# Half of v and k in fp32, the rest by casting loads, and two groups' heads taken to x first: the head of a linear-attention and gated-FFN kernel

## The chip, the cores and the metric

The kernel runs on one core of one Trainium2 chip. The metric is the device time of one execution in microseconds (us), the median of several runs. Five engines work side by side, each through its own list of instructions in order: TensorE (PE in the profile, its weight loads PEld), VectorE (DVE), ScalarE (ACT), GpSimd (POOL) and SyncE (SP). SP and POOL issue the transfers. In this kernel SP's loads keep their type, and POOL's loads convert on the way: fp32 in memory becomes bf16 or fp16 on the chip.

## What is computed

q, k and v are 8 batches x 8 heads x 576 positions x 64, in fp32. The attention is linear, without a softmax:

```python
def phi(x, c, s):
    r = np.maximum(x, 0.0)
    return np.concatenate([r * c, r * s], axis=-1)
q_p = phi(q, cos_w, sin_w)
k_p = phi(k, cos_w, sin_w)
kv = np.einsum('bhsf,bhsd->bhfd', k_p, v)
z = np.sum(k_p, axis=2)
num = np.einsum('bhsf,bhfd->bhsd', q_p, kv)
den = np.einsum('bhsf,bhf->bhs', q_p, z)[..., None] + 1e-06
x = (num / den)            # then 4608 tokens x 512
out = (silu(x @ w_gate) * (x @ w_val)) @ w_out
```

w_gate and w_val are 512 x 1536, w_out is 1536 x 512.

## The kernel before

**Tiles.** The 8 heads of a batch are taken as 4 groups of 2 (`g`), and these as 2 pairs of groups (`j`). A position is a partition p of 64 and a slot c of 9. A tile `t` of x is 128 tokens, two slots of one batch; four tiles make one token group of 512 for the feed-forward part, and there are 9 token groups. The hidden width 1536 is cut into 12 chunks of 128 (`fc`), the model width 512 into 4 (`kc`).

**Three stages.** The head (lines 133 to 563) loads the tables and batch 0 and takes the first four tiles through attention, then the first six chunks of the first token group through the gate (G) and value (V) products, silu (s) and their product (m). From L566 on jobs with costs and due times are planned in Python and put out in the planned order: the rest of the first token group, the other batches, the token groups 1 to 8 (with a scheme of seven products in place of eight on sums of blocks of x and of the weights) and the stores. The last stage ends with the stores of the last token group.

**What sets the order of the head.** The list `words` (L501) is an order written out by hand. Each word is one step, and the engine of a step gets its instructions in the order of the words: `tm` and `te` spread the tangents over the partitions and copy them out, `cq` casts two slots of q, `tq` turns a tile of q on TensorE, `qr` is its relu, `qw` its product with the tangents, `rk` the relu of k, `kv` the products of k with v times (cos, sin), `kvo` their copies to SBUF, `a` the products of a tile of q with kv, `den`, `rec` and `x` the denominator, its reciprocal and the quotient, `xt` and `xc` the turn of x on TensorE and the copy of it, `z` products of zeros with nobody to read them (`idle_products`, L184), `WG` and `WV` sums of weight blocks. A number behind the point is a part of a step or, for G, V, s and m, the tiles that it takes. `@act` and `@dve` choose the engine.

**PSUM.** Its 8 banks are handed out by `take`, the longest unused first; a bank that is held comes back with `give_back`. The planner's first assignment of banks (L1507) starts from the use in the head.

**Loads before.** SP issues six (L158 to L163, `load_first`): v of groups 0 and 1, v of groups 2 and 3, q slots 0 and 1, k of groups 0 and 1, and k of groups 2 and 3 in two parts (slots 0 to 4 and 5 to 8). They stay fp32 and lie in room that is used later for other things (`wo_sb`, `ht`, `wt_sb`). ACT casts v of groups 1 to 3 to bf16 (L461), DVE multiplies v of group 0 straight from fp32 (`vmul`, L293). POOL prepares constants, waits in a copy of one element (`hold`, L467) for the second group of v, and then issues casting loads: q slots 2 and 3, q slots 4 to 7, the first two chunks of w_gate and w_val, each 128 columns, and then the list of L472, larger pieces of the weights, batch 1, w_out and q of batch 2. At most eight of POOL's loads are on their way at a time; a ninth waits for the first.

## Time and profile before

| | us |
|---|---|
| median of 3 runs | 299.42 |
| lowest and highest | 298.96, 299.65 |
| the profiled execution | 298.21 |
| its span, first to last instruction | 296.4 |
| TensorE busy in it | 291.1 |

A line of the timeline begins with the start in us from the span's start and the time in us; then come engine, line of the program, operation, what is written and read, and how many instructions stand together. In brackets stand the idle time of the engine before it and what ended it. The chain of work that ended last is followed back from the last instruction; its pieces are given in order of time with start, length, engine and line. In the rows of slices a digit is a share in tenths. The DMA view gives what the transfers wrote in a stretch of time, and for each group of loads its size and the time from issue to landing.

### The profile page before, as it was taken

How to read it: one execution, taken by the hardware profiler on the slowest of the kernel's cores; microseconds unless marked ns; L12 is line 12 of the kernel's file. 1: busy time of each engine (PE TensorE's matmuls, PEld its weight loads, DVE VectorE, ACT ScalarE, POOL GpSimd, SP SyncE). 2: the span in 40 equal slices, each digit the busy share in tenths (PEclk: the TensorE clock that was granted, in tenths of full speed). 3: DMA queues.
4: the chain of work that ended last, by engine and by line, in shares of the span. 5: the costliest groups of instructions: out<-in, count | busy, mean ns of one | idle time of the engine just before them, and what ended most of it. 6: DMA issues, size and time to landing. Idle time of an engine off the chain costs nothing.

```text
span 296.4 us, 8073 instructions
## 1 busy us (share of the span) xinstructions
PE 291.1 (98%) x3244; PEld 238.7 (81%) x3244; DVE 252.0 (85%) x514; ACT 199.4 (67%) x421; POOL 69.6 (23%) x122
## 2 busy tenths in 40 slices
PE   8999999999999999999999999999999999999994
PEld 4597465776787888898898889888988888888883
DVE  7878997879877999999988987998679868986883
ACT  6564346989559968985699589967465556565630
POOL 7963630003007012221352023200220050002000
PEclk9999999999999999999999999999999999999999
DMA  7999999997989997799996979940470046002026
GB/s 266 225 196 198 202 206 207 203 205 121 194 177 144 229 190 122 151 171 149 174 203 133 186 113 162 183 81 2 107 110 2 0 97 119 2 0 73 0 58 157
DMA packets 71973, 40.89 MB, mean 138 GB/s; under 512 B 48768, under 2 KB 68736, under 8 KB 71936
## 3 DMA queue, kind: packets, MB, share of 16 engines
q0 software_dynamic: 24800, 24.39, 49.1%
q1 hardware_dynamic: 46528, 15.47, 28.9%
q10 hardware_dynamic: 608, 0.52, 0.7%
q8 instruction: 25, 0.41, 0.6%
q14 instruction: 12, 0.10, 0.1%
HBM read 37.75 MB, written 9.44 MB: 159 GB/s over the span
## 4 chain that ended last, share of the span: by engine, by line
PE 97%; DVE 1%; issue 0%
PE banks L977 45%; PE banks L1142 24%; PE banks L1052 5%; PE banks L1262 4%; PE banks L438 4%; PE banks L904 4%; PE banks L187 3%; PE banks L716 3%; PE banks L785 2%; PE banks L779 1%; PE banks L372 1%; PE banks L1310 0%; PE banks L315 0%; PE banks L418 0%; PE banks L351 0%
## 5 line engine op out<-in xcount | busy, mean ns | idle before, releaser
L1111 POOL DMA_DIRECT2D out_dram<-ob x52 | 27.3, 532 | 104.8 <-ACT ob L630 69.7
L1036 ACT ACTIVATE sg<-banks 128x512 bf16<-128x512 f32 x72 | 41.3, 599 | 5.6 <-PE banks L977 5.4
L977 PEld LDWEIGHTS <-wg_sb 128*128 128x128 f16 x384 | 36.9, 98 | 6.3
L628 ACT COPY banks<-banks 128x512 f32<-128x512 f32 (+1 forms) x53 | 29.9, 572 | 17.5 <-PE banks L977 7.3
L1142 PEld LDWEIGHTS <-ht 128*128 128x128 f16 x384 | 37.4, 98 | 4.8
L1072 DVE TENSOR_TENSOR ht<-sg,banks 128x512 f16<-128x512 bf16 x60 | 39.9, 680 | 0.9 <-PE banks L977 0.6
L977 PEld LDWEIGHTS <-wgs_sb 128*128 128x128 f16 x368 | 35.7, 98 | 4.6
L997 DVE TENSOR_TENSOR banks<-m,banks 128x512 f32<-128x512 f32 x44 | 30.2, 693 | 10.6 <-ACT m L628 8.1
L977 PEld LDWEIGHTS <-wv_sb 128*128 128x128 f16 x320 | 31.0, 98 | 3.8
L977 PE MATMUL banks<-kvt,wgs_sb 128*128 128x256 f16 x236 | 33.4, 273 | 0.0
L1142 PEld LDWEIGHTS <-sums 128*128 128x128 f16 x288 | 27.9, 98 | 3.3
L630 ACT ACTIVATE ob<-banks 128x512 f32<-128x512 f32 x32 | 18.8, 596 | 15.9 <-PE banks L1142 15.2
L977 PE MATMUL banks<-xT,wg_sb 128*128 128x256 f16 x192 | 28.8, 273 | 0.0
L628 ACT COPY m<-banks 128x512 f32<-128x512 f32 x44 | 25.5, 590 | 4.4 <-PE banks L977 4.3
L1142 PE MATMUL banks<-wo_sb,ht 128*128 128x256 f16 x192 | 25.7, 273 | 0.0
L1142 PE MATMUL banks<-wt_sb,sums 128*128 128x256 f16 x192 | 24.9, 273 | 0.0
L977 PE MATMUL banks<-xT,wv_sb 128*128 128x256 f16 x160 | 24.0, 273 | 0.0
L1036 ACT ACTIVATE sg<-m 128x512 bf16<-128x512 f32 x24 | 15.1, 630 | 12.4 <-DVE m L1005 12.2
L807 DVE TENSOR_TENSOR x<-banks,rec 128x512 f16<-128x512 f32 x32 | 21.6, 686 | 1.5 <-DVE rec L803 0.2
L977 PE MATMUL banks<-kvt,wg_sb 128*128 128x256 f16 x168 | 22.4, 273 | 0.0
L1142 PE MATMUL banks<-wt_sb,ht 128*128 128x256 f16 x192 | 22.3, 273 | 0.0
L877 ACT ACTIVATE r_q<-raw_q,tanq 128x256 bf16<-128x256 bf16 x45 | 20.7, 510 | 0.1
(160 smaller groups left out, 544.7 us busy)
## 6 DMA issues: line engine op xcount, KB each, us to landing
out_dram<-ob POOLq DMA_DIRECT2D x52, 128.0 KB, 3.9
raw_kv<-in_k_dram POOLq DMA_DIRECT2D x7, 576.0 KB, 5.9
raw_q<-in_q_dram POOLq DMA_DIRECT2D x12, 288.0 KB, 10.7
raw_kv<-in_v_dram POOLq DMA_DIRECT2D x6, 576.0 KB, 8.3
out_dram<-ob SPq DMA_DIRECT2D x12, 128.0 KB, 2.5
wg_sb<-in_moe_w_gate_dram POOLq DMA_DIRECT2D x5, 256.0 KB, 8.9
wv_sb<-in_moe_w_val_dram POOLq DMA_DIRECT2D x5, 256.0 KB, 9.5
wo_sb<-in_v_dram SPq DMA_DIRECT2D x2, 576.0 KB, 4.2
```

The lines of the kernel that those rows point to most:

```text
L438: nc.tensor.matmul(out=st["f", tg, fc, lo][i], lhsT=(wg_sb, wv_sb)[i][:, kc, fs], rhs=xT[tg][:, ts, kc], start=(kc == 0), stop=(kc == KC - 1))
L628: nc.scalar.copy(out=out, in_=in_)
L630: nc.scalar.mul(out=out, in_=in_, mul=mul)
L807: tt(out=one(x_all, x).rearrange("p (y e d) -> p e y d", e=2, d=D), in0=view()[:, :, :, 0:D], in1=rec_all[:, t % 4].rearrange("p (e y) o - ...
L877: nc.scalar.activation(out=home()[:, :, c, 1], in_=raws[b, "q"][:, :, c], func=AF.Relu, scale=tanq[:, c:c + 1])
L977: nc.tensor.matmul(out=to[:, i], lhsT=a[:, c, 2 * u + i], rhs=x()[:, :, c], start=first and i == 0 and c == 0, stop=c == KH - 1, skip_grou ...
L997: tt(out=bank(c), in0=one(m7_all, m).rearrange("p i x -> p (i x)"), in1=bank(b), op=ALU.add)
L1036: nc.scalar.activation(out=gates(rooms[w])[:, :, jh * HT:(jh + 1) * HT], in_=src, func=AF.Silu, scale=DOWN)
L1052: nc.tensor.matmul(out=bank(v), lhsT=wv_sb[:, kc, fc * P:(fc + 1) * P], rhs=xT[tg][:, :, kc], start=(kc == 0), stop=(kc == KC - 1))
L1072: tt(out=ht[:, 4 * u + w:4 * u + w + 3:2, jh * HT:(jh + 1) * HT], in0=gates(rooms[w])[:, :, jh * HT:(jh + 1) * HT], in1=src.rearrange("p ( ...
L1111: {"POOL": nc.gpsimd, "SP": nc.sync, "ACT": nc.scalar}[j.eng].dma_start(out=out_v[idx // NC, idx % NC][:, cols], in_=ob_of(t)[e * SH:(e + ...
L1142: nc.tensor.matmul(out=to, lhsT=a[:, kc, i * P:(i + 1) * P], rhs=b[:, kc], start=first and kc == 0 and i == 0, stop=kc == HC - 1, skip_gro ...
```

## The change

- v and k of groups 0 and 1 are still loaded by SP in fp32, now each group by itself: two loads of v and four of k (slots 0 to 4 and 5 to 8 of each group). ACT casts both groups of v (`vc`), and DVE multiplies from bf16 (`vm`).
- POOL's wait at L467 goes. POOL issues casting loads at once: q slots 0 to 3, v of groups 2 and 3, k of groups 2 and 3 in two parts, q slots 4 to 7. Behind them stand the weights and the list of before, word for word.
- q has no fp32 part any more: `cast_q` goes, and all turns of q read bf16 from the casting loads.
- Of the first 56 products of zeros 44 go; in the word list three remain (`z3`) of nine.
- The tangents are spread with both halves of the partitions, a diagonal of 320 columns instead of 640.
- Word list: the products kv, the copies, a, den, rec and x of groups 0 and 1 stand first, for tiles 0 and 1 (`HALVED`); then kv of groups 2 and 3, the turns of tiles 2 and 3, and the second halves of tiles 0 and 1. ACT makes the denominators of these four tiles. The first gate and value products take two tiles at once (`01`), and for chunk 0 the lower half of the model width (`Gl`, `Vl`) and the upper one (`Gh`, `Vh`) apart. The copy of x of tile 2 goes to DVE.
- The planner's first assignment of banks is written out (L1507); the order of what follows the word list on TensorE, VectorE, ScalarE and SyncE, and of what POOL issues behind the first weights, is that of before.

The diff, without its unchanged lines:

```diff
...
-    QCUT = 2
+    NW, QCUT = 8, 4
...
-    first = {"q": lodge(G * QCUT * D, FP32).rearrange("p (g c d) -> p g c d", g=G, c=QCUT)}
+    first = {}
...
-    load_first("v", slice(0, 2))
-    load_first("v", slice(2, 4))
-    load_first("q", slice(0, G), 0, 2)
-    load_first("k", slice(0, 2))
-    load_first("k", slice(2, 4), 0, KCUT)
-    load_first("k", slice(2, 4), KCUT, NC)
-    NW = 8
+    for g in range(2):
+        load_first("v", slice(g, g + 1))
+    for g in range(2):
+        load_first("k", slice(g, g + 1), 0, KCUT)
+        load_first("k", slice(g, g + 1), KCUT, NC)
...
-    idle_products(40, 16)
-    idle_products(4)
...
-    tan16 = consts.tile([P, NC + 1], FP16, name="tan16")
+    tan16 = consts.tile([SH, NC], FP16, name="tan16")
+    tan5 = consts.tile([P, (NC + 1) // 2], FP16, name="tan5")
...
-    diag = lodge((NC + 1) * SH, FP16).rearrange("p (c s) -> p c s", c=NC + 1)
+    epd_all = consts.tile([P, NC], FP32, name="eps_down")
+    NH2 = (NC + 1) // 2
+    diag = lodge(NH2 * SH, FP16).rearrange("p (c s) -> p c s", c=NH2)
+    eye2 = consts.tile([P, SH], FP16, name="eye2")
+    nc.vector.tensor_tensor(out=eye2, in0=ident16[:, 0:SH], in1=ident16[:, SH:P], op=ALU.add)
...
-        nc.vector.tensor_tensor(out=tan16[:, 0:NC], in0=csk[:, :, 1], in1=rcos[:, 0], op=ALU.mult)
-        nc.vector.tensor_copy(out=tan16[:, NC:], in_=tan16[:, 0:1])
+        for ps_, at, c0, n in ((slice(0, SH), 0, 0, NH2), (slice(SH, P), 0, NH2, NC - NH2), (slice(SH, P), NC - NH2, 0, 1)):
+            nc.vector.tensor_tensor(out=tan5[ps_, at:at + n], in0=csk[ps_, c0:c0 + n, 1], in1=rcos[ps_, 0, c0:c0 + n], op=ALU.mult)
...
+        nc.vector.tensor_single_scalar(out=epd_all, in_=rcos[:, 1], scalar=1e-6 * DOWN, op=ALU.mult)
...
-        nc.vector.tensor_tensor(out=diag[0:SH], in0=ident16[0:SH, 0:SH].unsqueeze(1).to_broadcast([SH, NC + 1, SH]),
-                                in1=tan16[0:SH].unsqueeze(2).to_broadcast([SH, NC + 1, SH]), op=ALU.mult)
+        nc.vector.tensor_tensor(out=diag, in0=eye2.unsqueeze(1).to_broadcast([P, NH2, SH]),
+                                in1=tan5.unsqueeze(2).to_broadcast([P, NH2, SH]), op=ALU.mult)
+        nc.vector.tensor_tensor(out=tan16, in0=csk[0:SH, :, 1], in1=rcos[0:SH, 0], op=ALU.mult)
...
-        nc.tensor.matmul(out=st["tan"][:, 0], lhsT=ones[0:SH], rhs=diag[0:SH, 0:NW].rearrange("p c s -> p (c s)"),
-                         start=True, stop=True)
-        nc.tensor.matmul(out=st["tan"][:, 1, 0:2 * SH], lhsT=ones[0:SH], rhs=diag[0:SH, NW:].rearrange("p c s -> p (c s)"),
-                         start=True, stop=True)
+        for h in range(2):
+            hs = slice(h * SH, (h + 1) * SH)
+            nc.tensor.matmul(out=st["tan"][:, h, 0:NH2 * SH], lhsT=ones[hs], rhs=diag[hs].rearrange("p c s -> p (c s)"),
+                             start=True, stop=True)
...
-        copy_op(eng, tanT.rearrange("p c s -> p (c s)"),
-                st["tan"].rearrange("p b x -> p (b x)")[:, 0:(NC + 1) * SH])
+        copy_op(eng, tanT.rearrange("p (h c) s -> p h (c s)", h=2), st["tan"][:, :, 0:NH2 * SH])
...
-        relu_op(eng, raw_of(0, "k")[:, g, lo:hi], first["k"][:, g, lo:hi])
+        o = raw_of(0, "k")[:, g, lo:hi]
+        relu_op(eng, o, first["k"][:, g, lo:hi] if g < 2 else o)
+
+    cast_v = set()
...
-            in0=(first if b == 0 and g == 0 else {"v": raw_of(b, "v")})["v"][:, g].unsqueeze(2).to_broadcast([P, NC, 2, D]),
+            in0=(first["v"] if b == 0 and g < 2 and g not in cast_v else raw_of(b, "v"))[:, g].unsqueeze(2).to_broadcast([P, NC, 2, D]),
...
-    qf = wgs_sb.rearrange("p n c u x -> p (n c u x)")[:, G * NC * 2 * W:G * NC * 2 * W + 4 * J * D].bitcast(
-        BF16).rearrange("p (c j i d) -> p c j i d", c=2, j=J, i=2)
...
-
-    def cast_q(c, eng):
-        o = qf[:, c % 2].rearrange("p j i d -> p (j i) d")
-        (nc.scalar.copy if eng == "act" else nc.vector.tensor_copy)(out=o, in_=first["q"][:, :, c])
...
-                if t == 0:
-                    nc.tensor.transpose(out=ps[:, y].rearrange("p e s -> p (e s)"),
-                                        in_=qf[:, c, j].rearrange("p i d -> p (i d)"), identity=ident)
-                    continue
...
-                    out=(ps[:, j, 2 * e * D1:2 * (e + 1) * D1] if t == 0 else
+                    out=(ps[:, j, 2 * e * D1:2 * (e + 1) * D1] if t in HALVED else
...
-        if t == 0:
+        if t in HALVED:
...
-    def x_den(t, ps, ys=slice(0, 4)):
-        if ys.start == 0:
-            st["den", t] = den_all[:, t % 4]
-        nc.vector.tensor_scalar(
-            out=st["den", t].rearrange("p (e y) o -> p e y o", e=2)[:, :, ys],
-            in0=a_view(t, ps, ys)[:, :, :, D:D1],
-            scalar1=eps_all[:, 2 * t:2 * t + 1], scalar2=DOWN, op0=ALU.add, op1=ALU.mult)
+    def x_den(t, ps, ys=slice(0, 4), eng=""):
+        st["den", t] = den_all[:, t % 4]
+        o, i_ = st["den", t].rearrange("p (e y) o -> p e y o", e=2)[:, :, ys], a_view(t, ps, ys)[:, :, :, D:D1]
+        if eng == "act":
+            nc.scalar.activation(out=o, in_=i_, func=AF.Identity, scale=DOWN, bias=epd_all[:, 2 * t:2 * t + 1])
+        else:
+            nc.vector.tensor_scalar(out=o, in0=i_, scalar1=eps_all[:, 2 * t:2 * t + 1], scalar2=DOWN,
+                                    op0=ALU.add, op1=ALU.mult)
...
-        if ys.start == 0:
-            st["rec", t] = rec_all[:, t % 4]
-            st["x", t] = x_all[:, t % NX]
+        st["rec", t] = rec_all[:, t % 4]
+        st["x", t] = x_all[:, t % NX]
...
+    HALVED = (0, 1)
...
-    def ffn_mm(tg, fc, lo=0, hi=GH, which=(0, 1)):
+    def ffn_mm(tg, fc, lo=0, hi=GH, which=(0, 1), ks=range(KC)):
...
-        if 0 in which:
+        if 0 in which and 0 in ks:
...
-            for kc in range(KC):
+            for kc in ks:
...
-                                 start=(kc == 0), stop=(kc == KC - 1))
+                                 start=(kc == 0 and (i == 0 or 2 * n > 512)), stop=(kc == KC - 1), skip_group_check=True)
...
+    def load_part(nm, gs, lo, hi):
+        nc.gpsimd.dma_start(out=raw_of(0, nm)[:, gs, lo:hi].rearrange("p g c d -> p g (c d)"),
+                            in_=source(0, nm)[:, gs, lo * D:hi * D])
+
...
-    for g in (0, 1, 2, 3):
-        if g:
-            nc.scalar.copy(out=raw_of(0, "v")[:, g], in_=first["v"][:, g])
-        vmul(0, g)
-        if g == 1:
-            tangent_diagonals()
-    hold = consts.tile([P, 1], FP32)
...
-    nc.gpsimd.tensor_copy(out=hold, in_=first["v"][:, 1, 0, 0:1])
-    load_slots(0, "q", QCUT, 4)
-    load_slots(0, "q", 4, NW)
+    load_part("q", slice(0, G), 0, QCUT)
+    load_part("v", slice(2, 4), 0, NC)
+    load_part("k", slice(2, 4), 0, KCUT)
+    load_part("k", slice(2, 4), KCUT, NC)
+    load_part("q", slice(0, G), QCUT, NW)
...
-    for what in "w2 w4 w6 k w8 s8 w10 v sa o002 o022 sb o044 o084 q2".split():
-        if what[0] == "w":
-            load_w(int(what[1:]))
-        elif what[0] == "o":
-            load_wo(int(what[1:3]), int(what[3:]))
-        elif what == "k":
-            load(1, "k")
-        elif what == "v":
-            load(1, "v", 2)
-        elif what[0] == "q":
-            load_turned(int(what[1:]), "q")
-        else:
-            load_slots(*{"s8": (0, "q", NW, NC), "sa": (1, "q", 0, 3), "sb": (1, "q", 3, NC)}[what])
+
+    def loads():
+        for what in "w2 w4 w6 k w8 s8 w10 v sa o002 o022 sb o044 o084 q2".split():
+            if what[0] == "w":
+                load_w(int(what[1:]))
+            elif what[0] == "o":
+                load_wo(int(what[1:3]), int(what[3:]))
+            elif what == "k":
+                load(1, "k")
+            elif what == "v":
+                load(1, "v", 2)
+            elif what[0] == "q":
+                load_turned(int(what[1:]), "q")
+            else:
+                load_slots(*{"s8": (0, "q", NW, NC), "sa": (1, "q", 0, 3), "sb": (1, "q", 3, NC)}[what])
...
-        tm0 te0@act cq1@act cq0@dve z4 rk1.0@dve rk0.0@act rk3.0@dve rk2.0@dve tq0 z2 rk3.1@dve kv0.0 qr0@act
-        kv1.0 qw0.1 rk2.1@act kvo01@dve kv1.1 tq1 kvo00@act kvo10@dve a0.0 kvo11@act qr1@dve z1 den0.0 qw1.1
-        a0.1 den0.1 tq3 rec0.0 rec0.1 tq2 a1.0 a1.1 z2 x0.0 qr3@act x0.1 den1 xt0.1 qw3.1 xt0.0 rec1 qr2@act
-        xc0.1@act qw2.1 a3.0 x1.0 a3.1 a2.0 den3 xc0.0@act a2.1 G1.0 xt1.0 rec3 G0.0 den2 x3.0 rec2 V0.0
-        xc1.0@act V1.0 s1.0 xt3.0 G0.1 G1.1 V0.1 x2.0 xc3.0@act xt2.0 xc2.0@act s0.1 s0.0 V1.1 G2.01 m0.0
-        s2.01 G3.01 m1.0 WG3.0 WG2.0 WG4.0 G1.23 G3.23 s1.23 V3.23 V1.23 G4.01 s1.1 s3.23 G0.23 m1.23 s3.01 m3.23 m1.1 m0.1
-        WV3.0 WV2.0 WV4.0 s4.01 s0.23 G4.23 G5.23 G2.23 s5.23 G5.01 V2.01 V2.23 V5.23 s4.23 V4.01 m2.01 m5.23 V4.23 s2.23 s5.01
-        m4.01 V3.01 V5.01 m2.23 V0.23 m4.23 m3.01 m5.01 m0.23
+        vc0@act td0 vm0 rk0.0@dve tm0 z3 tq0 vc1@act vm1 qr0@dve te0@act rk1.0@act kv0.0 qw0.1 kvo01@act tq1 vm2 qr1@dve kvo00@act qw1.1 a0.0 rk3.0@act den0.0@act rk2.0@act a1.0 vm3 rk2.1@dve den1.0@act rec0.0 rk3.1@act rec1.0 x0.0 kv1.0 kv1.1 x1.0 tq2 ld0 kvo11@dve kvo10@act tq3 a0.1 xt0.0 a1.1 qr3@act xc0.0@act qr2@dve qw2.1 xt1.0 den1.1@act den0.1@act qw3.1 xc1.0@act rec1.1 a2.0 rec0.1 x1.1 a2.1 den2@act a3.0 a3.1 x0.1 xt1.1 rec2 xt0.1 Gl0.01 xc1.1@act xc0.1@act den3@act x2.0 Vl0.01 G1.01 rec3 Gh0.01 V1.01 Vh0.01 x3.0 G3.01 xt2.0 xt3.0 G2.01 V2.01 xc3.0@act s2.01 WG3.0 xc2.0@dve G0.23 G1.23 s3.01 V1.23 G4.01 G4.23 s0.01 s0.23 s4.01 V0.23 s1.01 s4.23 V4.01 s1.23 m0.01 V4.23 WV3.0 WG2.0 G2.23 V2.23 m1.23 G3.23 m1.01 s2.23 m4.23 m0.23 V3.23 WV2.0 s3.23 m2.23 G5.23 m4.01 G5.01 s5.23 WG4.0 V3.01 WV4.0 V5.23 m3.23 m2.01 m3.01 s5.01 V5.01 m5.23 m5.01
...
-        whole, a, part = b not in ("0", "1") or a != "0", int(a), int(b or 0)
+        whole, a, part = b not in ("0", "1") or int(a) not in HALVED, int(a), int(b or 0)
...
-        elif op == "cq":
-            cast_q(a, eng)
+        elif op == "ld":
+            loads()
+        elif op == "vc":
+            copy_op(eng, raw_of(0, "v")[:, a], first["v"][:, a])
+            cast_v.add(a)
+        elif op == "vm":
+            vmul(0, a)
...
+        elif op == "td":
+            tangent_diagonals()
...
-            x_den(a, st["a", a], ys)
+            x_den(a, st["a", a], ys, eng)
...
-            if op in "GV":
-                ffn_mm(0, a, *span, which=("GV".index(op),))
+            if op[0] in "GV":
+                ffn_mm(0, a, *span, which=("GV".index(op[0]),),
+                       ks={"l": range(KC // 2), "h": range(KC // 2, KC)}.get(op[1:], range(KC)))
...
-    epd_all = consts.tile([P, NC], FP32, name="eps_down")
...
-        free["bank"] = [(t, n) for t, n in zip(BANK_AT, sorted(range(8), key=lambda x: used[x]))]
+        free["bank"] = [(t, n) for t, n in zip(BANK_AT, (0, 4, 5, 7, 2, 1, 6, 3))]
```

## The prediction

> **What bounds the kernel now.** The page comes first: its head, the slices, and the shares of the chain that ended last.
>
> ```profile
> span 296.4 us, 8073 instructions
> PE 291.1 (98%) x3244; PEld 238.7 (81%) x3244; DVE 252.0 (85%) x514; ACT 199.4 (67%) x421; POOL 69.6 (23%) x122
> PE   8999999999999999999999999999999999999994
> PEclk9999999999999999999999999999999999999999
> DMA  7999999997989997799996979940470046002026
> PE 97%; DVE 1%; issue 0%
> ```
>
> TensorE is busy in every slice, and the chain lies on it for 97% of the span. From the profile's end to the run's 298.21 us are 1.8 us that no engine row covers. The diff leaves the order of instructions after the word list as it was on every computing engine, so I ask one thing: when does the first planned product, L904, start? The chain in order of time, cut to that part, says what TensorE does until then.
>
> ```profile
> 0.99 6.88 PE banks L187 x56
> ...
> 10.34 0.65 PE banks L315 x30
> ...
> 13.09 0.57 PE banks L351 x16
> ...
> 14.23 0.43 PE banks L187 x2
> 14.66 0.22 PE banks L418 x4
> ...
> 14.95 1.04 PE banks L372 x15
> ...
> 18.34 8.96 PE banks L438 x84
> ```
>
> L187 is the products of zeros, which fill time. The real work starts near 10 us, and at 15 us the head products of a tile (L372) still stand in front of most feed-forward products (L438). From the timeline I take the pace of the latter and the end of the list:
>
> ```profile
> 18.40 1.91 PE L438 MATMUL banks<-xT,wg_sb 128*128 128x256 f16 x16
> 27.14 0.38 PE L904 MATMUL banks<-xT,wv_sb 128*128 128x512 f16 x1
> ```
>
> One such product lasts 0.27 us alone, so 16 in 1.91 us stand (1.91 - 0.27) / 15 = 0.109 us apart. The planned part starts at 27.14 us. What comes before 10 us waits for data, so the transfers are next: POOL's issues in the timeline, and the DMA view of three stretches.
>
> ```profile
> 2.48 0.81 POOL L179 MEMSET wt_sb<- 128x128 f16 x1
> 5.79 1.68 POOL L129 DMA_DIRECT2D raw_q<-in_q_dram  x2
> DMA packets 2299, 2.73 MB, mean 341 GB/s; under 512 B 501, under 2 KB 1531, under 8 KB 2299
> raw_q<-in_q_dram POOLq DMA_DIRECT2D x1, 256.0 KB, 5.7
> DMA packets 1816, 0.58 MB, mean 182 GB/s; under 512 B 1310, under 2 KB 1816, under 8 KB 1816
> DMA packets 4855, 1.91 MB, mean 191 GB/s; under 512 B 2246, under 2 KB 4853, under 8 KB 4853
> ```
>
> The stretches are 1.8 to 9.8 us (341 GB/s, nearly all fp32), 9.8 to 13 us (182) and 10 to 20 us (191). A casting load is counted by the bf16 or fp16 that it writes, so it reads twice that: 364 and 382 GB/s. Both kinds thus run at about one speed, and the head is a question of how many bytes stand ahead of what. The second q load is issued at about 6.7 us and lands 5.7 us later, at 12.35.
>
> **The change part by part.**
>
> *Loads.* Before, SP brings all of v and k and two slots of q in fp32, and POOL then casts six slots of q. After, SP brings v and k of groups 0 and 1 (four times 288 KB, the k ones each cut in two), and POOL casts q slots 0 to 3 (512 KB read), the rest of v (576), the rest of k (320 and 256) and q slots 4 to 7 (512). SP issues six loads either way; POOL issues five instead of two, 3 x 0.75 us more, but loses the copy of 1.37 us at L467 and its wait, and starts when its memset ends at 2.48 + 0.81 = 3.3 us instead of 5.79. So the weights are issued at about the same time. **Ahead of the last q load's end stand 3,328 KB in both kernels**: 2,304 of v and k and 1,024 of q. SP's 1.18 MB end at 1.8 + 1.18 / 0.341 = 5.3 us. In the old kernel the remaining 2.23 MB end about 0.9 us before 12.35 (the first load of v shows this lag: 0.59 MB at 341 GB/s end at 3.5, and the waiting cast starts at 4.45), that is in 6.15 us; as casting loads at 364 to 382 GB/s they need 5.8 to 6.1. I take 0.25 us of gain, from bounds of 0.0 and 0.35: **q slots 4 to 7 land at 12.1.**
>
> ```profile
> 4.45 0.67 ACT L461 CAST raw_kv<-wo_sb 128x576 bf16<-128x576 f32 x1 [0.64 <-DMA wo_sb<-in_v_dram]
> 69.26 0.75 POOL L121 DMA_DIRECT2D raw_kv<-in_k_dram  x1 [0.40 <-ACT den L797]
> DMA  9998300000000000099957711497999899999999
> q1 hardware_dynamic: 832, 1.11, 105.7%
> ```
>
> That needs the casting queue to be ready when SP's bytes run out. No row shows a casting load this early, so I bound it. With idle engines a load issued at 69.26 moves bytes at about 70.7 (slices of 0.1 us from 69): 1.45 us, hence 4.75 here, before 5.3. On the other side, between 5.8 and 8.8 us only q1, SP's queue, moved anything, though POOL issued at 5.79: 3.0 us, hence 6.3 and a hole of 1.0 us. I take no hole: SP's queue still held work then, so that row shows a turn awaited, not a delay of the load itself.
>
> *Order of the head.* q waits for nothing but its load (the two casts of L339 go), and k, v and the heads of groups 0 and 1 are done while the rest comes in. This removes 50 products of zeros. DVE makes all four products v*table from bf16, ACT makes the denominators (0.27 us each at L797), DVE one copy of x. The tangent set-up gains a few small operations and its diagonal halves; it lies before 6 us, where nothing waits for it longer than for q. None of this is on the path after 12.1, as DVE's and ACT's lists there hold only the following.
>
> ```profile
> 13.48 1.08 ACT L281 ACTIVATE wt_sb<-banks 128x512 bf16<-128x512 bf16 x2 [1.06 <-PE banks L351]
> 14.81 0.65 ACT L323 COPY xT<-banks 128x256 f16<-128x256 f16 x2 [0.24 <-PE banks L418]
> 42.12 0.27 ACT L797 ACTIVATE den<-banks,eps_down 128x8 f32<-128x8 f32 x1 [1.58 <-PE banks L779]
> 13.29 0.29 DVE L397 RECIPROCAL rec<-den 128x4 f32<-128x4 f32 x2
> 13.50 0.74 DVE L401 TENSOR_TENSOR x<-banks,rec 128x256 f16<-128x256 f32 x2
> ```
>
> *The path.* The turns of tiles 2 and 3 stand on TensorE ahead of the second halves of tiles 0 and 1, so these queue behind the landing. From 12.1: 16 transposes 0.57 and a hand-off 0.05; then ACT, in its order: the relu of tile 3 (1.08 / 2), the first xT copy (0.65 / 2), two denominators (0.27 each); then DVE's reciprocal (0.29 / 2) and the two half tiles (0.74); two more hand-offs 0.10, two transposes 0.11. Sum 3.1: the first gate products start at **15.2**. Behind them TensorE has 96 products of 0.109 (10.47) and 8 transposes of 0.22 / 4 (0.44): 26.1. I add 0.2 for a copy that ends 0.1 late behind the half-depth products and a bank not yet free: **26.3, a lead of 0.85 us** on 27.14. Cross-check: from 14.95 the old kernel has the same 96 products' worth (32 of its are half as wide), 15 head products (1.04) and 16 - 4 = 12 transposes (0.66), which gives its 27.1; the new one has 8 transposes (0.44), starts 0.25 later, and so ends 1.0 earlier if nothing waits.
>
> *What could take the lead back.* The weights and W_out are in the same order and bytes. The load of the second weight pair is issued at 10.45 and lands 6.4 later, at 16.85; the new order wants it 16 products (1.74) after 15.2, at 16.95, so it fits only just. W_out's third piece lands at 31.46 + 11.7 = 43.16 and is used at 44.24: 1.08 us of room for a lead of 0.85.
>
> ```profile
> wg_sb<-in_moe_w_gate_dram POOLq DMA_DIRECT2D x1, 256.0 KB, 6.4
> wo_sb<-in_moe_w_out_dram POOLq DMA_DIRECT2D x1, 512.0 KB, 11.7
> 44.24 1.03 PE L1262 MATMUL banks<-wo_sb,ht 128*128 128x512 f16 x4
> ```
>
> Sum: 298.21 - 0.85 = 297.4 for a run like the profiled one. The median of the runs is 299.42, 1.2 us above it; against it the forecast is 299.42 - 0.85 = **298.6 us**.
>
> **The rivals.**
>
> *A hole in the transfers.* If the first casting load comes 1.0 us after SP's bytes end, everything behind it lands 1.0 later, and the path hangs on it: 27.3 instead of 26.3, +0.15 us, **299.6**. For it: q1 alone between 5.8 and 8.8. Against it: the idle-queue row.
>
> *The clock drops (the one that is slower).* The weight loads of the idle products show the price:
>
> ```profile
> 4.81 0.15 PEld L187 LDWEIGHTS <-zeros 128*128 128x128 bf16 x1 [0.28 <-issue]
> 5.22 2.16 PEld L187 LDWEIGHTS <-zeros 128*128 128x128 bf16 x45 [0.26 <-issue]
> ```
>
> Until 5.2 us a product of 512 columns takes 0.43 us, later 0.43 / 2 (L187 x2 above), though PEclk says 9 throughout: TensorE needed 4.2 us of steady work to reach full speed. The new order drops 50 of the filling products and leaves gaps: by my sums the 15 products of zeros end near 6.6, and the first turn waits for q until 7.6 (5.3, then 0.52 MB at 373 GB/s, the middle of the two speeds, then the lag of 0.9); two more gaps of some 0.8 us follow before 12. If the speed falls there, the products from 15.2 on run at half for up to 4.2 us: 2.1 us lost against 0.85 won, **300.7**. It decides once more than 1.7 us of the dense part runs slow. Against it: none of the gaps is long, and TensorE works about half of that time. The Trainium skill ("TensorE: Matmul & The Clock Gate", section "HAM oscillation — how this bites in real kernels") asks for idle gaps above about 3.4 us before the clock falls; by that rule nothing is lost here and the sum stands. The next section of that page ("A second HAM failure mode: psum-queue depth-cycling") tells of many short gaps that did it in another kernel; by that one the time is the rival's. No row here shows a gap in the head of either length.
>
> *The lead isn't kept.* If the casting loads run at 364 and a little less, the weight pairs land 0.3 to 0.6 later than the new order wants them and TensorE waits: lead 0.3, **299.1**.
>
> **How the numbers follow.** A measurement of this kernel tells about 0.2%, 0.6 us, from no change. Forecast 0.54 (0.46 of it faster by more than that, 0.08 within); hole 0.18 (0.10 within, 0.08 slower, as a longer hole adds at once); clock 0.17 (0.02 within, 0.15 slower); lead not kept 0.11 (0.02 faster, 0.09 within). So faster 0.48, within 0.29, slower 0.23. The range goes from 297.8 (no waits, a full 0.35 from the transfers, 1.6 us in all) to 300.6, which takes in the hole and about half of the clock's case.
>
> **What would show it.** Right: the last q load lands near 12.1, the first gate product stands near 15.2, L904's successor starts near 26.3, and later stages are shifted by the same amount. Hole: q0's first packet after 6 us. Clock: 128x256 products 0.22 us apart after 15 us. Lead not kept: waits on weight loads between 16 and 21 us, or on W_out near 43. Wrong in kind would be a changed order after L904, or a slower stage beyond 60 us.

## The result, and the profile after

| | before | after |
|---|---|---|
| median of 6 runs, us | 298.99 | 305.38 |
| lowest and highest | 298.39, 299.65 | 301.76, 309.79 |
| the profiled execution, its span | 298.21, 296.4 | 306.81, 305.0 |

The change makes the kernel slower, by a little over 1%: ratio 1.013, 95% interval 1.009 to 1.017. (The ratio leaves out executions over 1.5% above a kernel's fastest; the medians do not.) The forecast of 298.6 us and its range of 297.8 to 300.6 were missed. What is new beside the time is the spread: 8 us between six runs of the changed kernel, 1.3 between six of the kernel before. (The old kernel isn't free of it: on the chip of a_third two of its 13 runs took 301.7 and 301.9 us, the others 298.0 to 299.1. They weren't traced.) The page of the profiled execution shows two places:

```profile
span 305.0 us, 7963 instructions
PE   8799999999999999999399999999999999999994
PEclk9799999999999999999899999999999999999999
PE 87%; DMA 8%; DVE 1%; POOL 1%; SPq 1%; issue 0%; POOLq 0%
```

TensorE's row, which before has nines between an 8 at the start and a 4 at the end, now has a 7 in the second slice and a 3 in the slice from 145 to 152.5 us. The chain, 97% on TensorE before, now runs through transfers for 8%. The head first, in the timeline of the changed kernel:

```profile
2.58 0.90 POOL L455 DMA_DIRECT2D raw_q<-in_q_dram  x1
...
9.19 0.41 PE L346 MATMUL banks<-ident,raw_q 128*64 128x128 bf16 x8 [1.76 <-DMA raw_q<-in_q_dram]
...
16.97 0.38 PE L434 MATMUL banks<-xT,wg_sb 128*128 128x256 f16 x2
...
19.42 0.61 PE L434 MATMUL banks<-xT,wg_sb 128*128 128x256 f16 x4 [0.54 <-DMA wg_sb<-in_moe_w_gate_dram]
...
28.61 1.03 PE L901 MATMUL banks<-xT,wv_sb 128*128 128x512 f16 x4
```

The first casting load is issued at 2.58, but TensorE waits 1.76 us for it until 9.19; the first gate product stands at 16.97, the second weight pair is waited for at 19.42, and the planned part (L901, once L904) starts at 28.61, 1.47 us later than before. The DMA view of the same kernel, stretch 4.5 to 8.5 us, and the issues of q slots 4 to 7 (at 5.60) and of the second weight pair (at 10.97):

```profile
q0 software_dynamic: 727, 0.49, 89.7%
q1 hardware_dynamic: 336, 0.33, 27.9%
...
raw_q<-in_q_dram POOLq DMA_DIRECT2D x1, 256.0 KB, 8.1
...
wg_sb<-in_moe_w_gate_dram POOLq DMA_DIRECT2D x1, 256.0 KB, 8.4
```

q0 is POOL's queue, which is counted by what it writes: 2 x 0.49 + 0.33 = 1.31 MB were read in these 4 us, where the old kernel read 1.47 MB. q slots 4 to 7 land at 5.60 + 8.1 = 13.7 us instead of 12.35.

The second place is the 3 in the row. TensorE's waits between 30 and 297 us (total, times, longest), and then the chain between 138 and 152 us (start, length, what):

```profile
PE banks L974 <- DMA xT<-x: 5.5, 1, 5.5
```

```profile
138.27 2.08 SPq L744
140.35 0.04 issue
140.39 9.66 DMA xT<-x
150.05 0.05 issue
150.10 1.04 PE banks L974 x4
```

The old kernel has no wait at all in the first of these views. Here SP issues the transposition of a tile of x at 140.39, it lands 9.66 us later, and all of TensorE's 5.5 us hang on it. It is tile 17, the last of three that SP issues in a row; POOL issues the k and v loads of batch 6 close by. First the kernel before, its timeline and then its DMA view, whose last number is the time to landing:

```profile
138.05 1.26 SPq L747 DMA_TRANSPOSE xT<-x  x1
139.69 0.79 POOL L121 DMA_DIRECT2D raw_kv<-in_k_dram  x1 [0.26 <-issue]
```

```profile
xT<-x SPq DMA_TRANSPOSE x1, 4.3
```

The same rows of the changed kernel's timeline (the landing stands in the chain above):

```profile
139.75 0.79 POOL L121 DMA_DIRECT2D raw_kv<-in_k_dram  x1
140.39 1.27 SPq L744 DMA_TRANSPOSE xT<-x  x1
```

Before, the transposition is issued 1.64 us ahead of the load; after, 0.64 us behind it. I call the distance the margin. Behind the wait the clock is low, as the windows view of the changed kernel says (granted clock ahead of the last two columns):

```profile
150.10:157.00 6.90, 6.90 (x49) 5.60 (x50) 4.99 (x10) 4.11 (x8) 0.00 (x0) 0.76 0.52 95
```

6.9 us at 0.76 are 1.7 us lost. With the wait of 5.5 and the head's 1.47 that makes 8.7, where the spans differ by 8.6.

### The profile page after: what moved, and what is told of

It reads as the page before. It is cut to its first block, busy times and chain, and to the rows that moved or that the text cites. A ratio compares the mean times of both kernels' runs of the same rounds, so it can differ in the third digit from the quotient of the medians.

```text
span 305.0 us, 7963 instructions
## 1 busy us (share of the span) xinstructions
PE 291.8 (96%) x3182; PEld 238.0 (78%) x3182; DVE 251.3 (82%) x512; ACT 198.8 (65%) x424; POOL 69.2 (23%) x124
## 4 chain that ended last, share of the span: by engine, by line
PE 87%; DMA 8%; DVE 1%; POOL 1%; SPq 1%; issue 0%; POOLq 0%
PE banks L974 43%; PE banks L1139 23%; PE banks L1049 5%; PE banks L1259 4%; PE banks L901 3%; DMA xT<-x 3%; PE banks L434 3%; DMA wg_sb<-in_moe_w_gate_dram 3%; DMA raw_kv<-in_v_dram 2%; PE banks L713 2%; PE banks L782 2%; PE banks L776 1%; SPq L744 1%; DVE ht L1069 1%; PE banks L1307 0%
## 5 line engine op out<-in xcount | busy, mean ns | idle before, releaser
L974 PEld LDWEIGHTS <-wg_sb 128*128 128x128 f16 x384 | 37.0, 98 | 12.2 <-DMA xT<-x 5.8
L1033 ACT ACTIVATE sg<-m 128x512 bf16<-128x512 f32 x24 | 15.1, 630 | 12.4 <-DVE m L1002 12.2
L298 DVE TENSOR_TENSOR v<-raw_kv,tab 128x1152 bf16<-128x1152 bf16 x28 | 20.6, 751 | 0.5 <-PE banks L782 0.3
```

The source lines that it names most:

```text
L298: nc.vector.tensor_tensor(out=v2s[b == 1][:, g, :, :, 0:D], in0=(first["v"] if b == 0 and g < 2 and g not in cast_v else raw_of(b, "v"))[: ...
L974: nc.tensor.matmul(out=to[:, i], lhsT=a[:, c, 2 * u + i], rhs=x()[:, :, c], start=first and i == 0 and c == 0, stop=c == KH - 1, skip_grou ...
L1033: nc.scalar.activation(out=gates(rooms[w])[:, :, jh * HT:(jh + 1) * HT], in_=src, func=AF.Silu, scale=DOWN)
```

## The experiments

The theory to be tested: **the head is late, because casting loads are slow at the start, and a small shift in the middle loses a race between a transposing DMA and casting loads.** The rivals: it is the clock; it is the order of the work or the banks; the loads are slow for another reason. The times of the experiments stand against the kernel before on the same chip, whose median was 298.5 to 298.8 us. The start is that of the planned part, 27.14 before.

| kernel | start, us | TensorE's longest waits behind 30 us | traced run | median (range), runs |
|---|---|---|---|---|
| changed | 28.61 | 5.5 tile 17 | 306.81 | 305.38 (301.76 to 309.79), 6 |
| a_again | 28.39 | none | 299.30 | |
| a_third | 29.52 | 4.2 tile 17 | 307.85 | |
| a_fourth | 26.88 | 1.8 tile 17 | 300.42 | |
| a_fill | 28.09 | 1.5 tile 17, 1.1 | 301.79 | 301.62 (301.09 to 304.40), 4 |
| a_xt_first | 29.54 | 1.1 tile 9, 0.6 | 303.14 | 303.25 (303.14 to 306.23), 4 |
| a_hold_v0 | 29.58 | 0.2 | 301.12 | 306.20 (301.12 to 311.14), 4 |
| a_early_q | 27.49 | 0.9, 0.5 | 300.02 | 301.05 (300.02 to 302.82), 6 |
| a_one_k | 28.02 | 0.9, 0.9 | 300.91 | 300.98 (298.15 to 302.14), 10 |
| a_fill_xt | 30.13 | 5.5, 0.7 | 309.65 | 308.27 (305.96 to 309.65), 4 |
| a_fill_x17 | 28.70 | 0.4 | 300.91 | 300.95 (300.91 to 303.80), 6 |
| a_early_x17 | 28.31 | 0.3 | 300.62 | 300.67 (300.20 to 305.49), 7 |
| b_late | 29.29 | 1.3 tile 9 | 302.19 | 300.43 (299.56 to 304.50), 10 |
| b_dma | 28.00 | none | 299.07 | 300.56 (299.07 to 302.83), 10 |
| b_race | 26.98 | 8.5 tile 17 | 308.42 | 309.04 (308.25 to 312.58), 4 |
| b_race_held | 27.34 | 1.4, 1.2, 1.0 | 304.98 | 304.70 (304.02 to 306.31), 4 |

### The changed kernel again (a_again, a_third, a_fourth)

No edit.

> The changed kernel once more, unchanged. Theory A (its loss is a head that is 1.5 us late and, run by run, other lost races of a transposing DMA against casting loads): again a planned part that starts 1.3 to 2.6 us late, but stalls at another place or of another length than 5.6 us at 150 us, and a time anywhere from 301 to 310 us. Rival B (the stall at 150 us belongs to the change's order): the same stall of 5 to 6 us again.

> The changed kernel unchanged, a third trace. Theory A (time = kernel before + late head + waits for transposed x or for loads in the middle): the span is 296.4 + (start of the planned part - 27.14) + TensorE's idle time behind 30 us + up to 1.7 us of slow clock behind a long wait, within 0.7 us. Rival B (something else in the changed kernel is slow in its long executions): the span is over 1 us more than this sum.

> The same once more: theory A, the same sum within 0.7 us; rival B, over 1 us more than the sum.

The first of the three shows no wait behind 30 us and a run of 299.30 us: one program, 7.5 us apart. Its race in the timeline, and in the DMA view:

```profile
139.20 1.49 SPq L744 DMA_TRANSPOSE xT<-x  x1
140.15 0.79 POOL L121 DMA_DIRECT2D raw_kv<-in_k_dram  x1 [0.38 <-PE banks L974]
```

```profile
xT<-x SPq DMA_TRANSPOSE x1, 3.1
```

Margin 0.95 us, landed after 3.1. In a_third the margin is -0.06 and the transposition takes 9.5 us, in a_fourth 0.20 and 6.6. Theory A of the first run is missed too (it expected a stall at another place and 301 us or more). Its rival B falls: the change's order, the same in all four, doesn't make the stall by itself. But three of the four traces lose this race, and the other five runs of the result weren't traced. The sum of theory A holds for a_again (a span of 297.4, against 296.4 + 1.25 = 297.65) and, at the edge of its 0.7 us, for a_fourth (298.6, against 296.4 - 0.26 + 1.8 = 297.9), but not for a_third by its own terms: 296.4 + 2.38 + 4.2 + 1.7 = 304.7, the span is 306.1. The windows view of a_third says what is missing, the clock behind the wait:

```profile
149.80:157.00 7.20, 7.20 (x41) 5.37 (x42) 4.62 (x10) 3.64 (x7) 0.00 (x0) 0.60 0.58 100
```

7.2 us at 0.60 are 2.9 us lost, not 1.7. With that the sum is 305.9.

The heads differ as well: 26.88 to 29.52 in four traces of one program, 26.98 to 27.34 in three traces of the old head (before, b_race, b_race_held). So a start that moves by half a us in one trace of an edited head shows nothing by itself.

### The race alone, in the kernel before (b_race, b_race_held)

```diff
+    aside = consts.tile([P, 2, KC, P], FP16, name="aside")
...
                 nc.sync.dma_start_transpose(out=xT_of(t), in_=one(x_all, x))
+                for n in range(2 if t == 18 else 0):
+                    nc.sync.dma_start_transpose(out=aside[:, n], in_=one(x_all, x))
```

and in b_race_held also

```diff
+            elif b == 6:
+                batch_loads(lambda: xT[4][0:1, 1, 0, 0:2], J_["turned", b - 1], names)
```

> The kernel before, its head untouched, but SP transposes tile 18's x twice more, into a spare tile that nobody reads, ahead of tile 17's. Each costs SP about 1.3 us, so tile 17's transposition is issued near 140.7 instead of 138.05 us, behind the k load of batch 6 (139.69) instead of 1.64 us ahead of it. Theory A (the late loss of the changed kernel is this lost race, nothing else in its code): tile 17 lands near 150 instead of 142.36, TensorE waits 5 to 7 us for it near 145, and the time is 304 to 307 us. Rival B (the stall needs the changed kernel's other landings or banks): a stall of at most 2 us and 299 to 301 us.

> The same with the two extra transpositions, and POOL's copy ahead of the k and v loads of batch 6 reads tile 17's transposed x, so that these loads come behind it by construction. Theory A (the order of the two decides, not the 2.6 us of SP's time): the stall is gone but for at most 1 us, and the time is 299 to 300.5 us. Rival B (SP's lost time itself is what costs): 303 us or more.

b_race gives ratio 1.036 (1.029 to 1.042), with the old head and the old code behind it. TensorE's waits, and the chain, both of b_race:

```profile
PE banks L981 <- DMA xT<-x: 8.5, 1, 8.5
```

```profile
141.64 9.68 DMA xT<-x
151.32 0.05 issue
151.37 1.04 PE banks L981 x4
```

This is the changed kernel's stall, at the same products, from a delay of SP by 3.6 us at one place (POOL's load is issued at 139.82, now 1.82 us ahead): theory A's mechanism holds, and the price is above its 304 to 307. Held behind the transposition, the loads give 304.70: the wait for tile 17 goes from 8.5 to 1.2 us, but the loads are issued at 145.10 instead of 139.8, and TensorE waits twice near 155. By its time this is rival B's case (303 us or more), not theory A's. What the trace shows is between the two: the order takes most of the stall away (8.5 to 1.2 us), and the loads have not 5 us to give.

### The same hold in the changed kernel (a_xt_first, a_fill_x17, a_early_x17, a_fill_xt)

The edit of b_race_held's second diff; `z10` for `z3` in the word list (in all but a_xt_first); the early q load of a_early_q (in a_early_x17). a_fill_xt holds batch 3's loads behind tile 9 too:

```diff
-                batch_loads(lambda: xT[2][0:1, 0, 0, 0:2], [J_["xT", 8]], names)
+                batch_loads(lambda: xT[2][0:1, 1, 0, 0:2], [J_["xT", 8]], names)
```

> The changed kernel, but POOL's small copy ahead of the k and v loads of batch 6 reads tile 17's transposed x instead of batch 5's turned q, so that these loads can't be issued before that transposition has landed. Theory A (the stall at 150 us is this transposition behind 1.2 MB of casting loads): no stall of over 1 us near 150, tile 17 lands within 3 us of its issue, and the time is that of before and the head's loss: 299.0 + 1.6 = 300.6 us, from 300.2 to 301.5. Rival B (TensorE waits there for something else, or the loads of batch 6, now 3 us later, are missed): 304 to 307 us, with a wait for them by 165 us.

> The changed kernel with ten products of zeros ahead of the first turn, and with the loads of batch 6 alone held behind tile 17's transposition (batch 3's are left as they were). Theory A (what is left is a head that is 1.0 to 1.3 us late, and smaller races at 77 and 92 us): no stall at 145 to 150 us, 299.7 to 301.5 us. Rival B (holding a load moves the loss to a later race, as holding batch 3's did): 303 us or more with a stall of over 2 us behind 150 us.

> The changed kernel with ten products of zeros, q slots 0 to 3 issued ahead of POOL's constants, and the loads of batch 6 held behind tile 17's transposition. Its planned part should start near 27.5 us, 0.35 behind that of the kernel before. Theory A: 299.0 + 0.4 = 299.4 us, up to 301 where the load of v for batch 3 is missed at 92 us; so no better than before. Rival B (something else in the middle of the changed kernel is slower): 301.5 us or more.

> The changed kernel with ten products of zeros ahead of the first turn instead of three, and with POOL's copies ahead of the loads of batches 3 and 6 reading tile 9's and tile 17's transposed x, so that neither race can be lost. Theory A (the head and these races are the whole loss): no stall of over 0.5 us at 77 and at 150 us, and 299.0 + 1.0 (the head with the products of zeros, 28.1 for 27.1) = 300.0 us, from 299.6 to 301.0, with little spread. Rival B (the loads, now 1 to 3 us later, are missed themselves): stalls at 92 or near 160 us and 301.5 to 304 us.

No trace of the changed kernel with batch 6 held shows a wait near 145 to 150 us. a_fill_x17 has its median at 300.95 and a_early_x17 at 300.67 us, ratios 1.009 (1.006 to 1.012) and 1.007 (1.005 to 1.009): within theory A's ranges, and neither beats the kernel before. a_early_x17 is there by another way than expected: its planned part starts at 28.31 instead of 27.5, and its trace shows no wait at 92 us. What the hold is worth isn't shown by the times: a_fill, the same head without it, has 301.62 us, and the ranges overlap. Nor is it clear why a_fill is 3.8 us below the changed kernel, for its head starts only 0.5 us earlier; in its trace the race is lost by 1.5 us instead of 5.5, with a margin of 1.0. a_xt_first missed its 300.2 to 301.5: its head was later still (29.54), and it lost the same kind of race, that of tile 9, at 77 us. a_fill_xt fell the other way: held for tile 9, the loads of batch 3 came 5 us later and met batch 3's own long transposition, which SP issued between k and v. The chain:

```profile
76.73 15.24 DMA raw_kv<-in_v_dram
91.97 0.02 issue
92.00 0.06 DVE v L298
...
93.48 1.67 PE banks L974 x7
```

The load of v took 15.2 us, and TensorE waited 5.5 us for what hangs on it. A hold that wins one race can lose the next.

### Late work and late loads, each alone, in the kernel before (b_late, b_dma)

```diff
-        ... a1.0 a1.1 z2 x0.0 ...
+        ... a1.0 a1.1 z10 x0.0 ...
```

and in b_dma

```diff
+    nc.gpsimd.dma_start(out=vsums.rearrange("p a b c d -> p (a b c d)")[:, 0:KC * 384].rearrange("p (c f) -> p c f", c=KC),
+                        in_=wg_r[:, :, 0:384])
     load_w(0, 1)
```

> The kernel before, with eight more products of zeros on TensorE ahead of the second half of tile 0, 8 x 0.216 = 1.73 us; nothing else moves, and no load is later. Theory A (the stall of 5.6 us at 150 us in the changed kernel comes from the later start alone: the transposing DMA of tile 17 is issued behind the k load of batch 6 instead of ahead of it): the same stall appears near 150 us, and the time is 303 to 309 us. Rival B (it needs the changed kernel's later landings, or its other order of banks): no stall at 150 us, and the time is 299.0 + 1.7 = 300.7 us.

> The kernel before, with one casting load more (768 KB read, 2.0 us at 382 GB/s, into a tile that is free then) between q and the weights, so that every later load lands about 2 us later, as in the changed kernel, while the order of the work is that of before. Theory A (landings that are late by 2 us make the head wait and lose races, whatever the order): the planned part starts 1.5 to 2.2 us late, stalls of 1 to 6 us appear behind 60 us, and the time is 301.5 to 306 us. Rival B (late landings cost only the head): 300.5 to 301.2 us.

Both come out by rival B: ratios 1.006 (1.005 to 1.008) and 1.006 (1.004 to 1.009). In the traces the planned part starts 2.15 and 0.86 us late, the medians are 1.7 and 1.9 us above the old kernel's, and tile 17's margins are 3.1 and 1.5 us. But b_late's trace loses the race of tile 9, with POOL's load issued 0.14 us ahead of the transposition, in the timeline and in the DMA view:

```profile
69.62 0.75 POOL L121 DMA_DIRECT2D raw_kv<-in_k_dram  x1 [0.40 <-ACT banks L628]
69.76 1.20 SPq L747 DMA_TRANSPOSE xT<-x  x1
```

```profile
raw_kv<-in_k_dram POOLq DMA_DIRECT2D x1, 576.0 KB, 6.8
...
xT<-x SPq DMA_TRANSPOSE x1, 6.9
```

So theory A, that the later start alone brings the stall at 150, isn't borne out: nine of b_late's ten runs took 302.2 us or less. Lateness makes such a loss possible, at whichever place its margin is used up.

### The start of the casting loads (a_hold_v0, a_early_q, a_one_k)

```diff
+    nc.gpsimd.tensor_copy(out=hold2, in_=first["v"][0:1, 0, 0, 0:2])
     load_part("q", slice(0, G), 0, QCUT)
```

In a_early_q, with `z10`, that load moves ahead of POOL's constants and SP's loads; in a_one_k, with `z10`, the two loads of k become one:

```diff
     KCUT = 5
+    load_slots(0, "q", 0, QCUT)
...
-    load_part("q", slice(0, G), 0, QCUT)
```

```diff
-    load_part("k", slice(2, 4), 0, KCUT)
-    load_part("k", slice(2, 4), KCUT, NC)
+    load_part("k", slice(2, 4), 0, NC)
```

> The changed kernel, with POOL waiting for the first load of v (landed at 3.68 us) before it issues its first casting load, so that this one moves its first bytes near 5.5 to 6 us instead of 4.5, when SP's fp32 bytes are nearly through. Theory A (two queues on the same DMA engines: while SP's last loads and POOL's first ran side by side, one engine fell 1.4 us behind, and every load since has landed that much late): SP's last part of k lands at 6.0 to 7.0 instead of 8.45, q slots 4 to 7 land at 12.2 to 12.8 instead of 13.70, the first planned product starts at 26.8 to 27.4 instead of 28.77, and the time falls to 298 to 300 us. Rival B (the bytes themselves are slow as casting loads at this place): the last q load lands no earlier than 13.7, or later by the shift of 1.3 us, 15.0, and the time is 305 us or more.

> The changed kernel with ten products of zeros ahead of the first turn, and its first casting load (q slots 0 to 3) issued ahead of POOL's constants, at about 0.8 instead of 2.6 us. Theory A (a casting load needs 1.2 us to its first bytes and 1.5 us more to full speed, and this ramp is what the change paid at 4.5 to 7.5 us): the ramp now lies beside SP's first loads, the first casting packets come near 2.5 to 3 us, 3328 KB are read by 11.6 to 11.9 us instead of 12.0 to 12.5, q slots 4 to 7 land at 12.5 to 13.1, and the planned part starts 0.4 to 0.9 us ahead of 28.09. Rival B (the casting loads are slow for another reason, such as two queues at once): q slots 4 to 7 land at 13.5 or later.

> The changed kernel with ten products of zeros ahead of the first turn and k of groups 2 and 3 as one casting load instead of two, so that the second weight pair is the ninth load behind q slots 0 to 3 (landed near 9.1 us) and no longer waits for v (10.7). Theory A (the ring held it back): it is issued near 9.6 instead of 10.9 us and lands by 18.3 instead of 18.85 to 19.4, the wait ahead of its first product is under 0.1 us, and the planned part starts at 27.6 to 27.9. Rival B (the bytes and one late engine decide): issued earlier, landed as before within 0.2 us.

a_hold_v0 refutes its theory A. SP's last part of k landed at 6.5 us as wished, so the queues hardly overlapped, and q slots 4 to 7 landed at 14.9: a later start of the casting loads is simply a later end. The sixteen engines still ended that load 2.2 us apart (12.70 to 14.92), so the spread doesn't need the two queues side by side. The median, 306.20, is rival B's too. What such a start costs is to be seen in the kernel before, where a casting load is issued at 69.26 with the DMA engines nearly free (last column GB/s written):

```profile
69.30:70.30 1.00, 1.00 (x9) 0.61 (x7) 0.96 (x4) 1.00 (x3) 1.00 (x2) 1.00 0.12 25
70.30:71.30 1.00, 1.00 (x6) 0.46 (x5) 1.00 (x2) 1.00 (x4) 1.00 (x2) 1.00 0.83 32
71.30:72.30 1.00, 1.00 (x8) 0.67 (x7) 1.00 (x3) 1.00 (x3) 0.69 (x2) 1.00 0.79 113
72.30:73.30 1.00, 1.00 (x7) 0.51 (x6) 1.00 (x3) 1.00 (x3) 0.00 (x0) 1.00 1.21 199
```

First bytes near 70.7, after 1.45 us, full speed after 3. a_early_q was to put this ramp beside SP's first loads. Its load is issued at 1.27 us, but POOL's queue moves no packet before 3.97, where 2.5 to 3 was expected. The 3,328 KB are read by 11.86 us, the last q load lands at 13.27 (expected by 13.1), and the planned part starts at 27.49, 0.60 ahead of a_fill. All three lie within what the unedited changed kernel did in its four traces (11.8 to 12.5, 12.7 to 14.2, 26.88 to 29.52), and a_early_x17, with the same head, starts at 28.31: so that the early load helps isn't shown. a_one_k shows the limit of eight loads on their way (the expectation's ring): the second weight pair is issued at 9.58 and lands at 17.88, TensorE no longer waits for it, and from the first gate product to the planned part it is 10.93 us. Its start is 28.02 nevertheless, 0.1 behind the expected range, with q at 13.6; ratio 1.005 (1.001 to 1.010).

### The clock (a_fill)

```diff
-        vc0@act td0 vm0 rk0.0@dve tm0 z3 tq0 ...
+        vc0@act td0 vm0 rk0.0@dve tm0 z10 tq0 ...
```

> The changed kernel, with ten products of zeros instead of three ahead of the first turn, 7 x 0.216 = 1.5 us of them, in the gap in which TensorE waits for q until 9.2 us. Theory A (the granted clock, 0.83 between 10 and 20 us, costs nothing: the path hangs on the landing of q slots 4 to 7): the first gate product and the first planned product start within 0.15 us of 16.97 and 28.77. Rival B (the clock is the loss of the head): they start 0.5 to 1.5 us earlier. The whole time falls by no more than that in either case; by A it stays at 302 to 309 us.

The gate products start 0.18 earlier, the planned part 0.52 (28.09 for 28.61; the expectation's 28.77 is the chain's figure for the same start). That looks like rival B's side, at its low end, but 0.34 of the 0.52 is a shorter wait for the second weight pair (0.20 instead of 0.54), which is a matter of transfers, and the rest lies within the spread of the unedited head. So a_fill doesn't show that the clock costs anything in this trace. The windows view of the changed kernel, of a_again, and of a_xt_first (granted clock before the last two columns):

```profile
10.00:13.00 3.00, 2.72 (x53) 2.13 (x47) 2.62 (x6) 1.64 (x5) 2.09 (x4) 0.50 1.56 185
```

```profile
10.00:13.00 3.00, 2.08 (x56) 1.33 (x45) 2.69 (x7) 1.94 (x7) 1.99 (x4) 1.00 1.46 185
```

```profile
13.00:17.00 4.00, 4.00 (x69) 3.24 (x67) 2.82 (x9) 1.91 (x5) 3.44 (x5) 0.50 1.69 185
```

After a gap of 1.76 us the clock fell to half in the first, after 1.55 it did not in the second. (In a_fill_xt it fell some 2 us behind a gap of 1.50, so no bound between these can be read.) In the first it was back before the last q load landed and cost little; in a_xt_first, after a gap of 3.3 us, it was not, and from that landing to the first gate product it took 4.6 us instead of 3.3. The same is to be seen in a_third, the changed kernel unedited: after a gap of 2.9 us the clock was at 0.50 from 8.8 to 15.6, and from the landing to the first gate product it took 4.4 us. So where the clock is still low at the landing, the path is over 1 us longer.

## Why the prediction was wrong, step by step

- **"so I ask one thing: when does the first planned product, L904, start?"** This is the step that failed. It takes the rest of the kernel as a constant. That "later stages are shifted by the same amount" was true of one of four traces of the changed kernel (a_again). In the first trace and in a_third 7 us were lost behind the head, at one race (waits of 5.5 and 4.2 us, and 1.7 and 2.9 us of slow clock); in a_fourth 2.5 us, 1.8 of them at the same race. With the rest constant the head's 1.47 us would have given 299.0 + 1.5 = 300.5 us, inside the range though on the wrong side: the landing of q, next, turned the sign, and the race made the size. The margins that the prediction worked out (the second weight pair, W_out's third piece) were those against a lead, between transfers and TensorE. The margin that decided, 1.64 us between SP's transposition and POOL's load, both off the path, stands in the trace of before and was not read.
- **"q slots 4 to 7 land at 12.1."** 13.7 in the first trace; 12.7 to 14.2 in the four. The bytes ahead were counted rightly. That the first casting bytes come at 4.75 was nearly right (4.87) by luck: the load was issued at 2.58, not 3.3, and took 2.29 us to its first packet, not 1.45. And 1.45 was wrong as a price, for from rest full speed came only after 3 us. So the rival of the hole had the right place, and its 1.0 us was near what was lost (1.35), but its 299.6 went by the same constant rest. The bytes account for 0.6 us of the 1.35: 3,328 KB were read by 12.0 instead of 11.4. The other 0.75 are a matter of spread: the sixteen engines end a load at 11.8 to 13.7 us after, at 11.3 to 12.35 before. Why they drift apart is open.
- **The path, "Sum 3.1".** 16.97 - 13.70 = 3.27: right.
- **The 96 products of 0.109, the transposes and 0.2 of waits, 11.1 in all.** 28.61 - 16.97 = 11.64; the 0.54 more is the wait at 19.42. The rival "the lead isn't kept" named that pair, but by a slower stream; a_one_k shows that it was the limit of eight loads, which held the issue until v had landed (10.97 instead of the 10.45 that the prediction left as it was). Head in sum: 1.60 + 0.17 + 0.54 = 2.31, from 26.3 to 28.61.
- **The clock.** "none of the gaps is long": the first, 1.0 us by the prediction's sums (6.6 to 7.6), was 1.2 to 2.9 us in the four traces. The Trainium skill ("TensorE: Matmul & The Clock Gate", section "HAM oscillation — how this bites in real kernels") asks for gaps above about 3.4 us; the first trace contradicts this with a fall after 1.76 us. The rival's price (2.1 us) was not paid in the dense part, which ran 0.11 us a product. In a_third over 1 us was paid ahead of it, and in both long traces the clock's price was paid, unforeseen, behind the lost race.
- **The chances.** 0.23 for slower by over 0.2% was too low. Each rival was a price at the head; none asked what else depends on when things happen.

What moves the margin is shown only in part. The load is released when batch 5's transposition has landed (12.2 us after its issue before, 10.5 after), and that one shares the engines with four stores of POOL. The DMA view of before (126.8 to 134 us), and of the changed kernel (128.6 to 136):

```profile
out_dram<-ob POOLq DMA_DIRECT2D x4, 128.0 KB, 7.7
phit<-r_q SPq DMA_TRANSPOSE x1, 12.2
```

```profile
out_dram<-ob POOLq DMA_DIRECT2D x4, 128.0 KB, 3.7
phit<-r_q SPq DMA_TRANSPOSE x1, 10.5
```

In the three traces of the unedited changed kernel that lost the race the stores were through in 3.7 us and the transposition in 10.2 to 10.9; in the fourth, a_again, the stores took 8.5. In before, b_late and b_dma the transposition took 12.2 to 12.5, with stores of 7.7 to 8.0. Where the stores go first, the loads of batch 6 are let go sooner and SP's third tile is not. That holds even in a_fourth, whose planned part started ahead of the old kernel's. The stores aren't all of it: in a_one_k they took 7.3 us and the transposition only 10.8, and the margin was still 1.15, as SP came to its third tile sooner. Why the changed head makes the stores go first so often wasn't settled.

## What to carry to other kernels

A tuned kernel with two DMA queues holds races that nobody wrote down: before moving a stage by a microsecond, list the pairs of transfers from different issuers that stand within 2 us of each other, and what is late if they swap. A short head is worth less than a steady one: the forecast gain was 0.85 us, the swing of the new head 2.6. And run the kernel several times before believing one trace: of four traces of this one program two show a loss of 7 us, one a small one and one none.

## What the runs showed of the hardware

- A transposition of 128 KB on SP's queue takes 3 to 5 us to land when issued 0.95 us or more ahead of casting loads (but 7.2 once, at a margin of 1.0), 6.6 at a margin of 0.20, and 9.5 to 9.7 when issued at the same time or behind them. It is not simply queued behind them: in the changed kernel its packets (q1) moved from 145 to 150 us beside POOL's,

```profile
q0 software_dynamic: 764, 0.84, 99.4%
q1 hardware_dynamic: 540, 0.13, 22.3%
```

  and hardly any (53 packets) in the 4.6 us before. The Trainium skill ("DMA: Bandwidth & Descriptors", section "Queues, rings and completion order") says that each engine takes the queues in turn, packet by packet. The last five us agree with it: from 145.4 to 148.9 the two queues moved 488 and 472 packets. The wait ahead of them it does not explain.
- A casting load from rest: first bytes 1.45 us after issue, 32 GB/s written in the second us, 113 in the third, 199 in the fourth. Beside SP's fp32 loads the first packet came later: 2.29 us after issue in the changed kernel, 2.70 in a_early_q.
- TensorE's granted clock fell to 0.50 after waits of 4.2 us and more (by 2.9 us of lost work in a_third), in the head after gaps of 2.9 to 4.3 us and once each after 1.76 and 1.50 us, in b_race_held after two waits of 1.4 and 1.0 us, and not after 1.55 us in the head or 1.8 us in the middle. The length of the gap alone does not decide. Each fall lasted 3.4 or 6.8 us (149.9 to 153.3 in the changed kernel, 148.7 to 155.5 in a_third), which is why a like wait cost 1.7 us in one and 2.9 in the other.
